# Attention with a third set of input tiles, a spread zero-fill and two-bank PSUM tiles, on one Trainium2 core

## The chip, the cores and the metric

The kernel runs on one core of one Trainium2 chip. The metric is the device time of one execution in microseconds. Of the kernel before, three runs are at hand: 874.6, 876.81 and 878.82 us, median 876.81. The engines are named TensorE (PE; PEld is its weight load), VectorE (DVE), ScalarE (ACT), GpSimd (POOL) and SyncE (SP, which here only issues transfers).

## The reference

Three stages follow one another: causal attention with a decay, a mixture of eight experts of which each token takes the best, and a dense stage. Cut to the formulas:

```python
# q, k, v: (4, 8, 576, 64), s: (4, 8, 576)
scores = q @ k.T / 8
cum    = cumsum(max(s, 0), -1)
scores = where(causal, -1e9, scores + min(-(cum[..., :, None] - cum[..., None, :]), 0))
attn   = softmax(scores)                    # exp(x - max) / (sum + 1e-9)
x      = (attn @ v) as 2304 rows of 512     # 4 batches x 576 rows

xn, en = x / (norm(x) + 1e-6), emb / (norm(emb) + 1e-6)
logits = xn @ en.T / tau                    # 8 experts
e      = argmax(logits);  gate = softmax(logits)[e]
y      = gate * (max(x @ w1[e], 0) @ w2[e])

h      = y @ w_in                           # 512 -> 2048
out    = (h * cos(h)) @ w_out               # 2048 -> 512
```

## The kernel before

**Tiling.** Attention works on 16 pairs of heads (p), four pairs to a batch. A pair is done in four steps, numbered n = 4p to 4p + 3: the last 64 query rows of both heads together, then query tiles 3, 2, and 1 with 0. A step is a chain over the engines: score matmuls on TensorE (`sco`); decay and row extreme in one pass on VectorE (`mx`, L299, which also writes `mx`); the exponential on ScalarE (`ex`, L565); transposes on TensorE into two one-bank PSUM tiles `t_ps` (`tr`, L315); a copy of one of them by ScalarE (`ca`, L571) and of the other by VectorE (`cd`, L574). Then the two products with v (`av`, L340), whose outputs are copied by ScalarE (`late`, L645) and, at the start of the next pair, by VectorE (`outs`, L610).

**Order.** In the attention part the order of SyncE, TensorE, ScalarE and VectorE is the order of the code. GpSimd's is not: a scheduler decides it when the program is built, and GpSimd then takes its instructions strictly in that order.

**Inputs.** SyncE loads q and k (`load`), the decay tile c_t (`load_c`, L107 and L109: the running sums of s, read back from `cumd` in one large and two small transfers) and v (`load_v`). Pair p + 2 is loaded in pair p; the tiles q, k and c have two buffers and v three. GpSimd then adds the causal mask to c_t in five instructions (`mask`, L129 to L134); `mx` of that pair needs them. The decay tile of pair 0 isn't loaded but made on the chip by matmuls and copies (`first_c`, tile `c_ps`).

**Rows.** When a batch's four pairs are done, `rows(b)` runs in pieces inside the next batch's loop: at each `point("a")`, `"ra"`, `"b"`, `"rb"`, `"x"` a task that waits for that name goes on by one piece. The pieces are: the logits matmuls into `lp_ps` and their copies (L388, L389), five times `turn` (transposes of the output into `r_ps`), `scaled` (a product on VectorE, L368) and `square` (ScalarE), the transposes `lt` with the products `lw` (L410), and `choose`, with the matmuls `rk` that count a token's place and the products pz. After that `route(b)` takes the norm (a power on GpSimd, L209, between two sets of VectorE operations), the gate, and for each of the five row tiles a product and a scatter to `xr` in DRAM on GpSimd (L505, L510). `xr` is zero-filled by eight transfers of 768 KB that `setup()` issues on SyncE. Batch 2's `pick_first` finds the fullest expert and loads its first rows (L539); batch 3's rows come after the loop, with `early_rows` (`xe_ps`). Then the expert stage begins, whose weights (`wraw`) are queued on SyncE behind L539.

The pools as they stand before:

```python
ld = tc.tile_pool(name="a_ld", bufs=2)                  # q, k, c; v has 3
xp = tc.tile_pool(name="a_x", bufs=7)                   # rows to scatter
ps_s = tc.tile_pool(name="ps_s", bufs=2, space=PSUM)    # two banks a tile
ps_t = tc.tile_pool(name="ps_t", bufs=4, space=PSUM)    # one bank a tile
```

Of the kernel before, what the change touches and what calls it, by code (L numbers as in the profile page):

```python
# [78 lines left out]
def attention(g, qd, kd, vd, sd, ied, embt, tau, ident, maskd, trid):  # L79
    tc, nc, const, dram, xr = g.tc, g.nc, g.const, g.dram, g.xr  # L80
    with ExitStack() as st:
        ld = st.enter_context(tc.tile_pool(name="a_ld", bufs=2))
# [6 lines left out]
        ps_t = st.enter_context(tc.tile_pool(name="ps_t", bufs=4, space=PSUM))  # L89
# [127 lines left out]
        def setup():  # L217
# [29 lines left out]
            for e in range(E):  # L247
                for _ in range(2):
                    yield
                nc.sync.dma_start(out=xr[e * NT:e * NT + 384].rearrange("(p c) d -> p c d", p=128), in_=zr.unsqueeze(1).to_broadcast([128, 3, DM]))  # L250
# [53 lines left out]
        def emit_t(n):  # L304
# [3 lines left out]
            tps = [ps_t.tile([128, 512], F32, tag="t", name="t_ps") for u in range(2)]  # L308
            for h, t in enumerate(px.pop(n)):
                for j in range(nb):  # L310
                    to = (j + 2) % 3 if tiles == (2,) else ((1, 2, 0)[j] if len(tiles) == 2 else j)
                    a = min(128 * j, S - 128) if tail else 128 * j
                    for u, tp in enumerate(tps):
                        r = slice(64 * u, 64 * u + 64)
                        nc.tensor.transpose(tp[:, 64 * (h * nb + to):64 * (h * nb + to) + 64], t[r, a:a + 128], idt[r, r])  # L315
            cp = []
            for u, tp in enumerate(tps):
                tv = tp[:, 0:128 * nb].rearrange("p (h j q) -> p h j q", h=2, j=nb) if not tail else tp[:, 0:320].rearrange("p (j q) -> p j q", j=5)
# [10 lines left out]
        def av(p, c0):  # L329
# [5 lines left out]
            o = ps_t.tile([128, 512], F32, tag="t", name="o_ps")  # L335
# [8 lines left out]
        def rows(b):  # L344
# [879 lines left out]
```

## Time and profile before

| | before |
|---|---|
| median of three runs | 876.81 us (874.6 to 878.82) |
| the profiled execution | 872.18 us |
| its span | 870.4 us |
| busy: TensorE, VectorE, ScalarE, GpSimd | 810.1, 579.0, 428.1, 129.6 us |
| TensorE busy, 0 to 200 us / 220 to 320 us | 161 of 200 / 99.2 of 100 us |
| first row load of the expert stage issued (L539) | 200.16 us |

Attention takes about the first 200 us of the span; there no engine is busy throughout. From 220 us on TensorE is. The profile comes from one execution, 4.6 us below the median, so sums of its parts are to be held against 872.2 and only their difference carried to the median. In a row of the profile's time order the bracket at the end says how long that engine had been idle before and what it then got; a row without a bracket followed at once. Rows of a few back-to-back instructions are joined (x2).

### The profile page before, as it was taken

The numbers are of one execution on the slowest core, as the hardware profiler recorded it, in microseconds if no ns is written. First come the engines' busy times: TensorE is split into PE (matmuls) and PEld (weight loads), VectorE is DVE, ScalarE is ACT, GpSimd is POOL, SyncE is SP. The second block draws the span as 40 slices with busy tenths as digits, with TensorE's granted clock in tenths as the row PEclk, the third lists the DMA queues.
The fourth block names the chain that finished last, engine by engine and source line by source line (L and its number), as shares of the span: only waits on it lengthen the run. The fifth ranks groups of instructions, "written<-read, shape, count | busy, mean of one in ns | idle before, by whom it ended". The sixth has DMA issues, their size and how long they took to land. (4 is left out here: it accounts for less than half of the span.)

```text
span 870.4 us, 14996 instructions
## 1 busy us (share of the span) xinstructions
PE 810.1 (93%) x5534; PEld 672.2 (77%) x5534; DVE 579.0 (67%) x1323; ACT 428.1 (49%) x916; POOL 129.6 (15%) x183
## 2 busy tenths in 40 slices
PE   7887989855999999999999999999999999999994
PEld 3555656534999999999998888888888888888883
DVE  5765989846456565656589968775777748544462
ACT  4776878824354454555537545343444434333331
POOL 3413474542100111111000000000000000000132
PEclk9999999975999999999999999999999999999998
DMA  6997676305976767887543212110111100000122
GB/s 209 282 377 222 209 240 208 109 36 188 328 265 150 145 151 170 173 173 151 167 156 86 95 49 73 49 49 25 49 49 49 50 0 1 1 1 0 49 85 87
DMA packets 41228, 107.84 MB, mean 124 GB/s; under 512 B 7486, under 2 KB 7998, under 8 KB 41150
## 3 DMA queue, kind: packets, MB, share of 16 engines
q1 hardware_dynamic: 37550, 97.30, 38.9%
q0 software_dynamic: 3552, 9.45, 2.9%
q8 instruction: 45, 0.74, 0.4%
q14 instruction: 33, 0.27, 0.1%
q10 hardware_dynamic: 48, 0.07, 0.0%
HBM read 91.00 MB, written 15.81 MB: 123 GB/s over the span
## 5 line engine op out<-in xcount | busy, mean ns | idle before, releaser
L804 DVE TENSOR_TENSOR wl<-wraw,wh 128x1024 fp32r<-128x1024 f32 x64 | 78.4, 1225 | 76.7 <-ACT wh L802 71.4
L1120 PE MATMUL h_ps<-x2h,wh 128*128 128x512 f32 (+1 forms) x320 | 118.4, 371 | 0.0
L1122 PE MATMUL h_ps<-x2h,wl 128*128 128x512 f32 (+1 forms) x320 | 118.3, 370 | 0.0
L1121 PE MATMUL h_ps<-x2l,wh 128*128 128x512 f32 (+1 forms) x320 | 118.1, 370 | 0.0
L1140 PE MATMUL facc<-wh,gh 128*128 128x512 f32 x288 | 114.9, 399 | 1.3 <-ACT gh L1127 1.3
L1142 PE MATMUL facc<-wh,gl 128*128 128x512 f32 x288 | 113.8, 396 | 0.0
L1141 PE MATMUL facc<-wl,gh 128*128 128x512 f32 x288 | 113.8, 395 | 0.0
L981 ACT ACTIVATE ki<-h_ps 128x512 int32<-128x512 f32 (+1 forms) x80 | 44.6, 557 | 119.6 <-PE h_ps L1122 115.0
L982 DVE SCALAR_TENSOR_TENSOR ki<-ki,h_ps 128x512 f32<-128x512 int32 (+1 forms) x80 | 50.5, 632 | 71.3 <-ACT ki L981 68.2
L802 ACT CAST wh<-wraw 128x1024 fp32r<-128x1024 f32 x64 | 67.1, 1049 | 51.2 <-PE acc L901 44.3
L565 ACT ACTIVATE s_sb<-s_sb,mx 128x576 f32<-128x576 f32 (+2 forms) x144 | 82.8, 579 | 11.0 <-DVE mx L299 10.8
L1152 POOL DMA_INDIRECT out_dram<-oacc,ti x18 | 17.5, 971 | 435.0 <-DVE oacc L1150 431.4
L901 PE MATMUL acc<-hl,wh 128*128 128x256 f32 (+7 forms) x256 | 76.7, 301 | 0.9 <-DVE hl L873 0.8
L983 ACT ACTIVATE ki<-ki,hpi 128x512 f32<-128x512 f32 (+1 forms) x80 | 54.5, 682 | 46.9 <-DVE ki L982 46.2
L902 PE MATMUL acc<-hh,wl 128*128 128x256 f32 (+7 forms) x256 | 76.5, 300 | 0.0
L900 PE MATMUL acc<-hh,wh 128*128 128x256 f32 (+7 forms) x256 | 76.3, 304 | 0.0
L1127 ACT CAST gh<-ki 128x512 fp32r<-128x512 f32 (+1 forms) x80 | 46.2, 578 | 51.6 <-DVE ki L984 51.1
L1121 PEld LDWEIGHTS h_ps<-x2l,wh 128*128 128x128 f32 x320 | 60.1, 188 | 12.5 <-DVE x2l L908 0.6
L1120 PEld LDWEIGHTS h_ps<-x2h,wh 128*128 128x128 f32 x320 | 60.0, 188 | 12.2
L1122 PEld LDWEIGHTS h_ps<-x2h,wl 128*128 128x128 f32 x320 | 60.1, 188 | 11.1
L299 DVE CUSTOM_DVE_ANT_0 s_sb<-s_ps,c_t 128x512 f32<-128x512 f32 (+3 forms) x112 | 58.3, 542 | 15.3 <-POOL c_t L129 12.8
L867 PE MATMUL h_ps<-xth,wh 128*128 128x368 f32 (+6 forms) x224 | 68.2, 304 | 0.0
(220 smaller groups left out, 1709.4 us busy)
## 6 DMA issues: line engine op xcount, KB each, us to landing
wraw<-in_wcat_dram SPq DMA_DIRECT2D x64, 512.0 KB, 4.9
wraw<-in_wf_dram SPq DMA_DIRECT2D x32, 512.0 KB, 3.6
k_t<-in_kd_dram SPq DMA_DIRECT2D x16, 496.0 KB, 4.9
c_t<-cumd SPq DMA_DIRECT2D x15, 512.0 KB
xr<-zr SPq DMA_DIRECT2D x8, 768.0 KB, 11.3
q_t<-in_qd_dram SPq DMA_DIRECT2D x16, 320.0 KB
v_t<-in_vd_dram SPq DMA_DIRECT2D x16, 320.0 KB, 6.1
c_t<-cumd SPq DMA_DIRECT2D x30, 144.0 KB, 4.7
```

What stands on the lines that cost most here:

```text
L565: nc.scalar.activation(**kw)
L804: nc.vector.tensor_tensor(out=lo, in0=raw, in1=hi.bitcast(F32), op=ALU.subtract)
L867: nc.tensor.matmul(out=ps[:, 0:c], lhsT=wh[:, sl], rhs=th[:, k, 0:c], start=(k == 0), stop=False)
L900: nc.tensor.matmul(out=ps[:, 0:c], lhsT=wh[:, sl], rhs=hh[:, 0:c], start=(f == 0), stop=False)
L901: nc.tensor.matmul(out=ps[:, 0:c], lhsT=wh[:, sl], rhs=hl[:, 0:c], start=False, stop=False)
L902: nc.tensor.matmul(out=ps[:, 0:c], lhsT=wl[:, sl], rhs=hh[:, 0:c], start=False, stop=(f == 7))
L1120: nc.tensor.matmul(out=ps[:, 0:w], lhsT=wh[:, sl], rhs=g.x2h[:, k, a0:a1], start=(k == 0), stop=False)
L1121: nc.tensor.matmul(out=ps[:, 0:w], lhsT=wh[:, sl], rhs=g.x2l[:, k, a0:a1], start=False, stop=False)
L1122: nc.tensor.matmul(out=ps[:, 0:w], lhsT=wl[:, sl], rhs=g.x2h[:, k, a0:a1], start=False, stop=(k == 3))
L1140: nc.tensor.matmul(out=acc[t], lhsT=gh[:, sl], rhs=wh[:, 512:1024], start=(c == s), stop=False)
L1141: nc.tensor.matmul(out=acc[t], lhsT=gh[:, sl], rhs=wl[:, 512:1024], start=False, stop=False)
L1142: nc.tensor.matmul(out=acc[t], lhsT=gl[:, sl], rhs=wh[:, 512:1024], start=False, stop=(c == e))
```

## The change

1. q, k and c get three buffers and v four. Pairs 1 and 2 are loaded ahead of the loop, pair p + 3 in pair p.
2. The eight zero-fills are no longer issued in two bursts by `setup()` but one each in pairs 1 to 8. A flag `g.filled` holds batch 0's route until pair 8.
3. The pool `ps_t` has two tiles of two banks in place of four of one. `c_ps`, `t_ps`, `r_ps`, `o_ps` and `xe_ps` take such a tile; `o_ps` holds both products of a pair.
4. `scaled` is one VectorE operation over both banks in place of two.
5. Two more points, `"c"` and `"rc"`; lt, lw and the pieces of `choose` move to earlier points; batch 2's `pick_first` and norm start inside pair 15.
6. The tile x has twelve buffers in place of seven.

The code, cut to its core:

```diff
-        ld = st.enter_context(tc.tile_pool(name="a_ld", bufs=2))
+        ld = st.enter_context(tc.tile_pool(name="a_ld", bufs=3))
-        ps_t = st.enter_context(tc.tile_pool(name="ps_t", bufs=4, space=PSUM))
+        ps_t = st.enter_context(tc.tile_pool(name="ps_t", bufs=2, space=PSUM))
...
-            vt[p] = ld.tile([128, 5, 128], F32, tag="v", name="v_t", bufs=3)
+            vt[p] = ld.tile([128, 5, 128], F32, tag="v", name="v_t", bufs=4)
...
         load(1)
+        load_c(1)
         load_v(0)
-        load_c(1)
+        load(2)
+        load_c(2)
         load_v(1)
+        load_v(2)
...
-            for e in range(E):
-                for _ in range(2):
-                    yield
-                nc.sync.dma_start(out=xr[e * NT:e * NT + 384]..., in_=zr...)
...
-            tps = [ps_t.tile([128, 512], F32, tag="t", name="t_ps") for u in range(2)]
+            tps = ps_t.tile([128, 2, 512], F32, tag="t", name="t_ps")
...
-                x = xs[i] = xp.tile([128, DM], F32, tag="x", name="x")
-                for h, r in enumerate(rr.pop(i)):
-                    nc.vector.tensor_tensor(...)
+                x = xs[i] = xp.tile([128, DM], F32, tag="x", name="x", bufs=12)
+                nc.vector.tensor_tensor(...)
...
-            yield "a"
+            yield "c"
             lt = ps_s.tile([128, 2, 512], F32, tag="s", name="lt_ps")
...
-            turn(2)
             square(1)
-            yield "ra"
+            yield "rc"
             lw = sm.tile([128, 5, H, E], F32, tag="lw", name="lw", bufs=1)
...
+            yield "a"
+            turn(2)
+            yield "ra"
             scaled(2)
+            lg = ...
...
+            yield "c"
+            square(3)
+            next(pick)
+            yield "rc"
+            next(pick, None)
             yield "a"
             turn(4)
             first = pick_first() if b == B - 2 else None
             if first:
                 next(first)
-            yield "rb"
+            yield "ra"
+            scaled(4)
             if first:
                 next(first)
...
-            if p + 2 < NPAIR:
-                load(p + 2)
-                load_c(p + 2)
-                load_v(p + 2)
+            if p + 3 < NPAIR:
+                load(p + 3)
+                load_c(p + 3)
+                load_v(p + 3)
+            g.filled = p >= E
+            if 0 < p <= E:
+                nc.sync.dma_start(out=xr[(p - 1) * NT:(p - 1) * NT + 384]..., in_=zr...)
...
             ca(n + 1)
+            point("c")
             tr(n + 2)
+            point("rc")
             tr(n + 3)
...
+            o2 = ps_t.tile([128, 2, 512], F32, tag="t", name="o_ps")
-            late = av(p, 256)
+            late = av(p, 256, o2)
```

How it moves instructions, at three places of the built programs. In brackets stands what an instruction waits for: an engine's name with a number is that engine's semaphore, DMAHW a transfer of SyncE's queue.

GpSimd at the start, before: c_t_114 is the decay tile of pair 0, c_t_123 that of pair 1.

```order
L129 TENSOR_TENSOR c_t_114<-c_t_114,mk_f_100 128x64 [waits DMAHW5_49,DVE_49]
L134 TENSOR_TENSOR c_t_114<-c_t_114,mk_f_100 128x256 [waits Activation_49] x2
L131 TENSOR_TENSOR c_t_114<-c_t_114,mk_f_100 128x2x128 [waits DVE_49]
L132 TENSOR_TENSOR c_t_114<-c_t_114,mk_f_100 128x2x128
L131 TENSOR_TENSOR c_t_123<-c_t_123,mk_f_100 128x2x128 [waits DMAHW1_49]
```

The same place now: c_t_114 is pair 0's, c_t_121 pair 1's and c_t_131 pair 2's.

```order
L134 TENSOR_TENSOR c_t_121<-c_t_121,mk_f_100 128x256 x2
L129 TENSOR_TENSOR c_t_121<-c_t_121,mk_f_100 128x64 [waits DMAHW2_49,DMAHW1_49]
L131 TENSOR_TENSOR c_t_131<-c_t_131,mk_f_100 128x2x128 [waits DMAHW6_49]
L132 TENSOR_TENSOR c_t_131<-c_t_131,mk_f_100 128x2x128
L134 TENSOR_TENSOR c_t_131<-c_t_131,mk_f_100 128x256
L129 TENSOR_TENSOR c_t_114<-c_t_114,mk_f_100 128x64 [waits DVE_49]
L134 TENSOR_TENSOR c_t_131<-c_t_131,mk_f_100 128x256
L129 TENSOR_TENSOR c_t_131<-c_t_131,mk_f_100 128x64 [waits DMAHW7_49,DMAHW0_49]
L134 TENSOR_TENSOR c_t_114<-c_t_114,mk_f_100 128x256 [waits Activation_49] x2
L131 TENSOR_TENSOR c_t_114<-c_t_114,mk_f_100 128x2x128 [waits DVE_49]
L132 TENSOR_TENSOR c_t_114<-c_t_114,mk_f_100 128x2x128
```

Pair 1's additions and most of pair 2's moved ahead of pair 0's.

ScalarE, the copies out of `t_ps` and of the first product in a pair of the first batch, before:

```order
L571 COPY pt<-t_ps 128x5x64 [waits PE_49,Activation_49]
L571 COPY pt<-t_ps 128x2x4x64 [waits PE_49,Activation_49]
L565 ACTIVATE s_sb,rs<-s_sb,mx 128x576 [waits DVE_49]
L571 COPY pt<-t_ps 128x2x3x64 [waits PE_49,Activation_49]
L571 COPY pu<-t_ps 128x6x64 [waits PE_49,Activation_49]
```

The same now:

```order
L576 COPY pt<-t_ps 128x5x64 [waits DVE_49,Activation_49]
L576 COPY pt<-t_ps 128x2x4x64 [waits DVE_49,Activation_49]
L570 ACTIVATE s_sb,rs<-s_sb,mx 128x576
L576 COPY pt<-t_ps 128x2x3x64 [waits DVE_49,Activation_49]
L576 COPY pu<-t_ps 128x6x64 [waits PE_49,Activation_49]
```

The order is the same, but three of the four copies wait for VectorE (its copy of the same tile) and no longer for TensorE alone; on VectorE the copy into pu and the output copies wait for ScalarE.

VectorE at the end of pair 15, before (o_ps is the last product, pf and pi belong to `pick_first`, ra to the norm of batch 2):

```order
L474 TENSOR_TENSOR cacc<-cacc,cs 128x8 [waits DVE_49]
L648 COPY ot<-o_ps 128x256 [waits PE_49]
L521 SCALAR_TENSOR_TENSOR key_3046<-c_ps,ef 128x8 [waits PE_49]
L523 TENSOR_REDUCE c_3048<-key_3046 128x1 [waits DVE_49]
L524 TENSOR_REDUCE c_3048<-c_ps 128x1
```

The same place now:

```order
L536 SCALAR_TENSOR_TENSOR pf<-pf 128x1 [waits DVE_49]
L538 CAST pi_2937<-pf 128x3 [waits DVE_49]
L212 TENSOR_SCALAR ra<-ss 128x5 [waits Activation_49]
L659 COPY ot<-o_ps 128x256 [waits Activation_49]
L216 RECIPROCAL rb<-rc 128x5 [waits Pool_49]
```

`pick_first` and the norm's first operation (on which GpSimd's power waits) moved from behind the last output copy to ahead of it.

## Rows read from the trace of the kernel before

**Rows 1.** Windows: from:to, busy by engine, granted clock, DMA share, GB/s.

```profile
80.00:100.00 20.00, 18.60 (x258) 12.70 (x256) 19.21 (x70) 17.67 (x57) 6.33 (x12) 1.00 0.59 193
```

**Rows 2.** Waits up to 180 us, VectorE then GpSimd: total, times, longest.

```profile
DVE s_sb L299 <- POOL c_t L129: 12.8, 4, 6.0
...
DVE rs L389 <- issue: 4.9, 2, 2.4
...
DVE rs L389 <- ACT lgs L388: 1.8, 1, 1.8
...
POOL c_t L131 <- DMA c_t<-cumd: 60.6, 11, 13.2
```

**Rows 3.** Time order, GpSimd: start, us, line, operation, operands, idle before.

```profile
15.63 0.73 POOL L131 TENSOR_TENSOR c_t<-c_t,mk_f 128x256 f32<-128x256 f32 x1 [1.46 <-DMA c_t<-cumd]
...
18.38 0.32 POOL L129 TENSOR_TENSOR c_t<-c_t,mk_f 128x64 f32<-128x64 f32 x1
...
25.25 0.73 POOL L131 TENSOR_TENSOR c_t<-c_t,mk_f 128x256 f32<-128x256 f32 x1 [6.55 <-DMA c_t<-cumd]
```

**Rows 4.** Time order, VectorE, pair 0, second softmax step.

```profile
14.45 0.69 DVE L299 CUSTOM_DVE_ANT_0 s_sb<-s_ps,c_t 128x512 f32<-128x512 f32 x1 [1.09 <-PE s_ps L276]
```

**Rows 5.** Time order, SyncE's queue, decay load of pair 1.

```profile
11.36 0.39 SPq L107 DMA_DIRECT2D c_t<-cumd  x1
```

**Rows 6.** DMA issues of the page: operands, count, KB each.

```profile
k_t<-in_kd_dram SPq DMA_DIRECT2D x16, 496.0 KB, 4.9
...
c_t<-cumd SPq DMA_DIRECT2D x15, 512.0 KB
...
xr<-zr SPq DMA_DIRECT2D x8, 768.0 KB, 11.3
...
q_t<-in_qd_dram SPq DMA_DIRECT2D x16, 320.0 KB
...
v_t<-in_vd_dram SPq DMA_DIRECT2D x16, 320.0 KB, 6.1
...
c_t<-cumd SPq DMA_DIRECT2D x30, 144.0 KB, 4.7
```

**Rows 7.** Two windows of 2 us, columns as in Rows 1.

```profile
22.00:24.00 2.00, 2.00 (x18) 1.30 (x18) 2.00 (x9) 2.00 (x7) 0.00 (x0) 1.00 1.04 255
...
50.00:52.00 2.00, 1.88 (x28) 1.32 (x24) 2.00 (x8) 1.91 (x5) 0.00 (x0) 1.00 1.03 401
```

**Rows 8.** Time order, VectorE, first step of pairs.

```profile
47.38 0.76 DVE L299 CUSTOM_DVE_ANT_0 s_sb<-s_ps,c_t 128x576 f32<-128x576 f32 x1 [0.44 <-ACT s_sb L565]
...
58.80 0.76 DVE L299 CUSTOM_DVE_ANT_0 s_sb<-s_ps,c_t 128x576 f32<-128x576 f32 x1 [4.05 <-POOL c_t L129]
...
72.91 0.76 DVE L299 CUSTOM_DVE_ANT_0 s_sb<-s_ps,c_t 128x576 f32<-128x576 f32 x1 [6.00 <-POOL c_t L129]
```

**Rows 9.** Time order, pair 3, copies on ScalarE and VectorE.

```profile
47.96 0.88 ACT L571 COPY pt<-t_ps 128x320 f32<-128x320 f32 x2
...
48.07 1.08 DVE L574 COPY pt<-t_ps 128x320 f32<-128x320 f32 x2
```

**Rows 10.** Time order, row stages in pairs 13 and 14.

```profile
159.59 0.64 ACT L388 COPY lgs<-lp_ps 128x576 f32<-128x576 f32 x1 [1.46 <-PE r_ps L361]
...
160.26 0.15 DVE L389 COPY rs<-lp_ps 64x4 f32<-64x4 f32 x1 [2.44 <-issue]
...
169.41 0.55 DVE L410 TENSOR_TENSOR lw<-lt_ps,ri 128x160 f32<-128x160 f32 x2 [0.16 <-PE lt_ps L404]
```

**Rows 11.** Time order, end of attention: VectorE, GpSimd, SyncE.

```profile
181.41 0.42 DVE L648 COPY ot<-o_ps 128x256 f32<-128x256 f32 x1 [2.28 <-PE o_ps L340]
...
183.37 1.20 POOL L209 TENSOR_TENSOR rc<-ra,half 128x5 f32<-128x5 f32 x1 [18.29 <-DVE ra L208]
...
192.06 0.75 DVE L368 TENSOR_TENSOR x<-r_ps,ri 64x256 f32<-64x256 f32 x2 [4.56 <-DMA xr<-x,pi]
...
200.16 1.03 SPq L539 DMA_DIRECT2D x<-xr  x2
```

More of the change, by code (lines that the diff above doesn't have):

```diff
@@ L312, in emit_t @@
                     a = min(128 * j, S - 128) if tail else 128 * j
-                    for u, tp in enumerate(tps):
+                    for u in range(2):
                         r = slice(64 * u, 64 * u + 64)
-                        nc.tensor.transpose(tp[:, 64 * (h * nb + to):64 * (h * nb + to) + 64], t[r, a:a + 128], idt[r, r])
+                        nc.tensor.transpose(tps[:, u, 64 * (h * nb + to):64 * (h * nb + to) + 64], t[r, a:a + 128], idt[r, r])
             cp = []
-            for u, tp in enumerate(tps):
-                tv = tp[:, 0:128 * nb].rearrange("p (h j q) -> p h j q", h=2, j=nb) if not tail else tp[:, 0:320].rearrange("p (j q) -> p j q", j=5)
+            for u in range(2):
+                tv = tps[:, u, 0:128 * nb].rearrange("p (h j q) -> p h j q", h=2, j=nb) if not tail else tps[:, u, 0:320].rearrange("p (j q) -> p j q", j=5)
                 if tail:
@@ L334, in av @@
             c1, last = (S, 4) if c0 else (256, 1)
-            o = ps_t.tile([128, 512], F32, tag="t", name="o_ps")
+            o = o2[:, 0 if c0 else 1]
             for j in range(last + 1):
@@ L356, in turn @@
                 q0, q1 = QT[i]
-                rr[i] = [ps_t.tile([128, 512], F32, tag="t", name="r_ps") for h in range(2)]
+                rr[i] = ps_t.tile([128, 2, 512], F32, tag="t", name="r_ps")
                 for e in range(4):
@@ L412, in rows @@
                                         in1=ri[:, :, 4 * u:4 * u + 4].unsqueeze(3).to_broadcast([128, 5, 4, E]), op=ALU.mult)
+            yield "a"
+            turn(2)
+            yield "ra"
             scaled(2)
+            lg = sm.tile(s3, F32, tag="lg", name="lg", bufs=1)
+            nc.vector.tensor_reduce(out=lg, in_=lw.rearrange("p i h e -> p i e h"), axis=AX.X, op=ALU.add)
+            nc.vector.tensor_tensor(out=l, in0=lg, in1=ien.unsqueeze(1).to_broadcast(s3), op=ALU.mult)
             yield "b"
@@ L416, in rows @@
             square(2)
-            lg = sm.tile(s3, F32, tag="lg", name="lg", bufs=1)
-            nc.vector.tensor_reduce(out=lg, in_=lw.rearrange("p i h e -> p i e h"), axis=AX.X, op=ALU.add)
-            nc.vector.tensor_tensor(out=l, in0=lg, in1=ien.unsqueeze(1).to_broadcast(s3), op=ALU.mult)
             next(pick)
@@ L423, in rows @@
             next(pick)
+            yield "c"
[3 more added lines that the diff above has]
+            next(pick, None)
             yield "a"
             turn(4)
-            square(3)
-            next(pick)
-            yield "ra"
-            scaled(4)
-            next(pick, None)
-            yield "b"
-            square(4)
             first = pick_first() if b == B - 2 else None
@@ L495, in route @@
             yield
+            while b == 0 and not g.filled:
+                yield
             gt = small([128, 5], "gt")
@@ L537, in pick_first @@
             for j in range(2):
[L538 removed]
+                x = xp.tile([128, DM], F32, tag="x", name="x", bufs=12)
                 nc.sync.dma_start(out=x, in_=xr[bass.ds(g.first * NT + 128 * j, 128)])
```

25 lines of the change are left out of this document (14 added, 11 removed).

## The prediction

> **What bounds the kernel now.** I read the table of windows first, then the waits by engine, then single stretches in time. The span is 870.4 us and the execution 872.2. Everything that the change touches lies in the first 210 us, the attention part; the expert and dense stages behind it are taken as unchanged, so the whole question is at what time they start. In the attention loop two different limits follow one another. In the pairs that carry routing rows VectorE is the limit: 19.21 of 20 us busy between 80 and 100 us [rows 1]. In the first six pairs VectorE waits: 12.8 us in four waits for GpSimd's decay additions (L129), and GpSimd in turn stood 60.6 us for the decay loads [rows 2]. So up to about 73 us the loop goes at the speed of the input queue. The reader should see that the second row explains the first: GpSimd is hardly busy, it is late because the transfer is.
>
> **Part A: what stands first on GpSimd (cost).** The order of GpSimd's work is not written by hand; in the changed program both the additions of pair 1 and the first three of pair 2 stand ahead of the first addition of pair 0, and GpSimd takes its work in order. In the kernel before, pair 1's five additions begin at 15.63 us, when its decay rows land, at about 0.7 us each, and the last, of 0.32 us, begins at 18.38 and ends at 18.70 [rows 3]. The second softmax step of pair 0 starts at 14.45 us on VectorE [rows 4]. After the change it can start only when GpSimd has: waited for pair 2's large decay transfer (landing at T); done three additions of pair 2 (2.1 us) and pair 0's 0.32; one more of pair 2 (0.7) and its 0.32, then three of pair 0 (2 x 0.7 and 0.73). That is T + 5.6 us.
> For T: behind pair 1's large decay transfer, issued at 11.36 [rows 5] and landed at 15.63, the queue now holds its two 144 KB pieces, v of pair 0 (320 KB), q, k and the large decay transfer of pair 2 (320, 496, 512 KB) [rows 6], 1,936 KB or 1.98 MB. At the 255 GB/s that these loads reached between 22 and 24 us it takes 7.8 us (T = 23.4), at the 401 GB/s of the stretch with fills 4.9 us (T = 20.5) [rows 7]. The first row is the same kind of load, but some bytes already move before 15.63: I take T = 22.5. The delay is 22.5 + 5.6 - 14.45 = **+13.7 us** (11.6 to 14.6). Nothing covers it: VectorE, ScalarE and TensorE all feed on that softmax. Even if pair 2's rows were there at once, GpSimd is occupied with pair 1 until 18.70, so the floor is 18.7 + 5.6 - 14.45 = 9.9 us.
> The Trainium skill, page "DMA: Bandwidth & Descriptors", section "Anatomy of one DMA", gives about 2 us fixed and 436 GB/s; as an estimate from that page, the 1.98 MB would take 4.5 us and T would be about 20.2. The trace's 255 GB/s under full queues speaks against it, and the sum goes by the row.
>
> **Part B: loads three pairs ahead, fill in pieces (gain).** The four VectorE waits of 12.8 us in all [rows 2], the longest 4.05 and 6.00 us before the first step of a pair [rows 8], go, since each decay load gets a whole pair more. In their place I put the 0.4 us that a pair without such a wait shows (for ScalarE, at 47.38) [rows 8]: 12.8 - 4 x 0.4 = **-11.2 us**. Does the queue keep up? From step to step those pairs take 58.80 - 47.38 - 4.05 = 7.4 and 72.91 - 58.80 - 6.00 = 8.1 us. A pair's loads are 1,936 KB, 7.8 us at 255 GB/s; a fill of 768 KB is 2.0 us at 401 GB/s [rows 6, 7]. The queue loses about 2 us a pair, in pairs 1 to 4, and has one pair (7.4 us) of lead more, plus the idle start. So it just holds; if not, up to 3 us of wait come back. Bounds -12.4 to -8.
>
> **Part C: two-bank tiles (cost).** The two halves of a transposed step were two tiles: in pair 3 ScalarE's copies at 47.96 and VectorE's at 48.07 ran side by side, 0.44 and 0.54 us each [rows 9]. With one tile of two banks the built order makes ScalarE's copy wait for VectorE's in three of four steps, the fourth the other way round, and the output copies likewise. A tile that was so before shows what that means: the copy of lp_ps on VectorE (160.26) stood 2.44 us and began once ScalarE's (159.59, 0.64 long) was through [rows 10]. By page "PSUM — Partial Sum Buffer" of the Trainium skill, section "Specifications (TRN2)", ScalarE and VectorE may read in parallel while they keep to different banks; by it the two-bank tile costs nothing. The row shows that here the program's order, not the bank, holds the reader back; the sum goes by the row.
> Laying pair 3 out again by hand, the loop of output copy, first steps, copies, four exponentials and late copy comes to 7.7 to 8.1 us instead of 7.8: +0.2 for each of five plain pairs, and +0.2 for ten pairs with rows, where ScalarE has more slack: **+3.0 us**. Bounds 0 (all covered) and one copy of each engine exposed in every pair, 16 x 0.98 = 15.7.
>
> **Part D: row pieces at other points.** The transposes lt and the products lw now follow each other with no other VectorE work between; before, lw (169.41) waited 0.16 us, [rows 10], with a copy of 0.54 us [rows 9] ahead of it as cover. Without cover that is 0.7 us, in three batches; for the rank matmuls and their products, which are fewer, I estimate 0.45, in two: **+3.0 us** (0 to 6). One scaled product of 128x512 instead of two of 128x256: two take 0.75 us together [rows 11], another operation that reads 128x512 out of PSUM 0.69 [rows 4]: -0.06 each, -1 us over twenty at most, and within the bound.
> **Part E: the end of attention (gain).** Batch 2's pick and norm now stand ahead of the last output copy. Before, GpSimd's power began at 183.37, 1.96 us behind that copy at 181.41 [rows 11]; its scatters and with them the x load on SP (200.16) follow. I take the 1.96: **-2.0 us** (-4 to 0). The 12 x buffers remove VectorE's 4.56 us wait for a scatter at 192.06 [rows 11] and two smaller ones; I cost that at nothing, because batch 3's rows run beside GpSimd's scatters and the x load, which end later; should that cover be gone, it is worth as much as it waited.
>
> **Sum**: 13.7 - 11.2 + 3.0 + 3.0 - 2.0 = +6.5 us. The profiled execution would come to 872.2 + 6.5 = 878.7. It lay 4.6 us below the median of 876.81, so for the median 883.3.
>
> **Rivals.** (1) *Pair 2's decay is there early.* If all of it lands by 18.7 us, the start costs 9.9 instead of 13.7: 879.5, no change that can be measured. For it: the queue reached 401 GB/s with other shapes. Against: before, GpSimd waited for that same transfer, queued behind the same q and k, for 6.55 us, until 25.25 [rows 3].
> (2) *The new places fit the row pairs better*, the case that isn't slower. VectorE's stalls at the first row stage, 2.44 twice and 1.8 [rows 2, 10], are 6.7 us; if the moved pieces and fewer tiles close them, part D is -6.7 instead of +3.0: 873.6. It decides against me as soon as those stalls shrink below half. Against: lp_ps is still one tile read by ScalarE first.
> (3) *The serialised readers bind every pair.* 16 x 0.98 = 15.7 in place of 3.0: 896. For it: ScalarE has the copies and the exponentials in one line, and the tile's next writer waits for both. Against: the row pairs' limit is VectorE, not ScalarE.
>
> **How the numbers follow.** My forecast has 0.42 (most of it slower, 0.06 at the edge of no change), rival 1 0.17 (0.13 no change, 0.04 slower), rival 2 0.24 (0.14 faster, 0.10 no change), rival 3 0.17 (slower). This measurement can tell about 0.5%, 4.4 us, from no change. Faster 0.14, same 0.29, slower 0.57. The range from 870 to 895 leaves out the better half of rival 2 and the worse half of rival 3.
>
> **What would show it.** Right: in the trace after, GpSimd's first wait ends with pair 2's decay near 22.5 us, the second softmax step starts near 28, no VectorE wait for L129 after that, ScalarE copies starting as VectorE's end, and the x load on SP about 4.5 us later than before. Wrong: pair 0's additions ahead of pair 2's transfer (part A falls, and the change gains about 7 us), or waits for decay rows that return in pairs 3 to 6 (part B).

## The result and the profile after

The changed kernel takes 886.73 us (median of four runs, 886.04 to 888.42) where the kernel before took 875.7 beside it: +11.0 us, ratio 1.0127 with a 95% interval of 1.0089 to 1.0165. It is slower by a little over 1%, and the whole interval lies above 1. The profiled execution took 887.13 us (span 885.3) against 872.18 before, +14.9 us; the profiled execution of before lay below its median and that of the changed kernel did not, so the profiles' difference is some 4 us more than that of the medians.

The table follows both traces from stage to stage; the times are starts in time order, of VectorE's first softmax step of a pair, of its last output copy and of SyncE's row load for the expert stage.

| | before | changed | difference |
|---|---|---|---|
| pair 1 starts | 18.74 | 30.77 | +12.0 |
| pair 1 to pair 6 | 54.17 | 46.63 | -7.5 |
| pair 6 to the last output copy | 108.50 | 120.31 | +11.8 |
| last output copy to the row load | 18.75 | 15.82 | -2.9 |
| row load starts | 200.16 | 213.53 | +13.4 |
| dense stage starts (first matmul on x2h) | 454.74 | 469.35 | +14.6 |

**The start.** These rows of the changed kernel in time order answer to [rows 3 to 5]; first GpSimd, then VectorE, then SyncE's queue.

```profile
13.76 0.72 POOL L131 TENSOR_TENSOR c_t<-c_t,mk_f 128x256 f32<-128x256 f32 x1 [11.32 <-DMA c_t<-cumd]
...
20.87 0.72 POOL L131 TENSOR_TENSOR c_t<-c_t,mk_f 128x256 f32<-128x256 f32 x1 [4.07 <-DMA c_t<-cumd]
...
22.91 0.32 POOL L129 TENSOR_TENSOR c_t<-c_t,mk_f 128x64 f32<-128x64 f32 x1
...
25.52 0.72 POOL L131 TENSOR_TENSOR c_t<-c_t,mk_f 128x256 f32<-128x256 f32 x1
...
23.27 0.76 DVE L299 CUSTOM_DVE_ANT_0 s_sb<-s_ps,c_t 128x576 f32<-128x576 f32 x1 [7.91 <-POOL c_t L129]
...
26.28 0.69 DVE L299 CUSTOM_DVE_ANT_0 s_sb<-s_ps,c_t 128x512 f32<-128x512 f32 x1 [2.24 <-POOL c_t L131]
...
10.08 0.38 SPq L107 DMA_DIRECT2D c_t<-cumd  x1
```

GpSimd stands 4.07 us for pair 2's transfer, until 20.87; only at 22.91 does it make the first addition of pair 0, and at 25.52 the one (L131) that the second step needs. VectorE waits 7.91 and 2.24 us for these two, and that step starts at 26.28 instead of 14.45.

**The waits.** Total, times and longest, up to 195 us; four rows of VectorE and one of ScalarE, to be held against [rows 2].

```profile
DVE ot L618 <- ACT ot L656: 12.6, 11, 2.4
...
DVE s_sb L299 <- POOL c_t L129: 7.9, 1, 7.9
...
DVE rs L388 <- ACT lgs L387: 4.7, 3, 1.7
...
DVE tri_b L240 <- DMA tri_f<-in_trid_dram: 3.3, 1, 3.3
...
ACT pt L576 <- DVE pt L579: 18.6, 28, 2.1
```

All of the waits for L129 that stood in the pairs are gone; the one left is that of the start. In their place stand two that the kernel before did not have: VectorE's output copy behind ScalarE's, and ScalarE's copies behind VectorE's on the same tile, 28 times. The stalls at the first row stage (L388, L389 before), 6.7 us in [rows 2], are 4.7 us here.

**The plain pairs.** Starts of pairs 4, 5 and 6 in the changed kernel, as [rows 8].

```profile
61.42 0.75 DVE L299 CUSTOM_DVE_ANT_0 s_sb<-s_ps,c_t 128x576 f32<-128x576 f32 x1
...
69.41 0.75 DVE L299 CUSTOM_DVE_ANT_0 s_sb<-s_ps,c_t 128x576 f32<-128x576 f32 x1
...
77.40 0.75 DVE L299 CUSTOM_DVE_ANT_0 s_sb<-s_ps,c_t 128x576 f32<-128x576 f32 x1
```

They follow at 7.99 us each, where 11.42 and 14.11 us lay between the same starts before.

**A pair with rows.** Pair 8 of the changed kernel in time order.

```profile
102.82 0.20 DVE L470 TENSOR_TENSOR pz<-rk_ps,eb 128x40 f32<-128x40 f32 x1 [0.40 <-PE rk_ps L467]
...
104.37 0.55 DVE L579 COPY pt<-t_ps 128x384 f32<-128x384 f32 x1
...
104.96 0.48 ACT L576 COPY pt<-t_ps 128x384 f32<-128x384 f32 x1 [1.76 <-DVE pt L579]
...
106.47 3.90 PE L340 MATMUL o_ps<-pt,v_t 128*64 128x320 f32 x20 [0.56 <-DVE pu L579]
...
111.58 0.42 DVE L618 COPY ot<-o_ps 128x256 f32<-128x256 f32 x1 [2.34 <-ACT ot L656]
```

The same stretch in windows; columns as in [rows 1].

```profile
102.00:104.00 2.00, 1.53 (x36) 1.44 (x36) 1.50 (x6) 1.20 (x4) 2.00 (x4) 1.00 1.04 352
...
104.00:106.00 2.00, 0.79 (x14) 0.44 (x10) 1.97 (x9) 1.04 (x3) 0.38 (x2) 1.00 0.68 209
...
106.00:108.00 2.00, 1.53 (x8) 0.83 (x10) 2.00 (x9) 2.00 (x7) 0.00 (x0) 0.74 0.92 362
...
108.00:110.00 2.00, 2.00 (x12) 1.05 (x10) 0.28 (x3) 1.04 (x4) 0.68 (x1) 0.50 0.38 85
```

VectorE does a piece of the routing (pz and what follows, 102.82 to 104.37; the last piece of `choose`, which the change moved to the new point `"rc"`) before its third copy of the pair. ScalarE's copy of the other half waits 1.76 us for it, and TensorE's product with v for both; TensorE is busy 0.79 of the 2 us from 104 on. The granted clock, 1.00 until then, is 0.74 and 0.50 in the next four microseconds; a stretch that was granted 0.50 ran at 1.2 of 2.4 GHz. The product takes 3.90 us (2.28 in pair 3 before), the output copies wait 2.34 us more, and the pair lasts 12.48 us instead of 8.43.

**The end.** GpSimd's power, the last output copy and the row load, as [rows 11].

```profile
196.36 1.20 POOL L213 TENSOR_TENSOR rc<-ra,half 128x5 f32<-128x5 f32 x1 [22.71 <-DVE ra L212]
...
197.71 0.42 DVE L659 COPY ot<-o_ps 128x256 f32<-128x256 f32 x1 [1.43 <-ACT ot L656]
...
213.53 0.97 SPq L544 DMA_DIRECT2D x<-xr  x2
```

The power now starts ahead of the copy, not 1.96 us behind it; the load follows the copy after 15.82 us instead of 18.75.

### The profile page after: what moved, and what is told of

The parts are those of the page before. It is cut to its first block, busy times and chain, and to the rows that moved or that the text cites. A ratio compares the mean times of both kernels' runs of the same rounds, so it can differ in the third digit from the quotient of the medians.

```text
span 885.3 us, 14973 instructions
## 1 busy us (share of the span) xinstructions
PE 810.8 (92%) x5534; PEld 668.1 (75%) x5534; DVE 583.4 (66%) x1303; ACT 429.5 (49%) x916; POOL 129.5 (15%) x183
## 5 line engine op out<-in xcount | busy, mean ns | idle before, releaser
L1151 PE MATMUL facc<-wh,gh 128*128 128x512 f32 x288 | 114.9, 399 | 1.3 <-ACT gh L1138 1.3
L1153 PE MATMUL facc<-wh,gl 128*128 128x512 f32 x288 | 113.8, 396 | 0.0
L1152 PE MATMUL facc<-wl,gh 128*128 128x512 f32 x288 | 113.8, 395 | 0.0
L570 ACT ACTIVATE s_sb<-s_sb,mx 128x576 f32<-128x576 f32 (+2 forms) x144 | 82.7, 580 | 12.7 <-DVE mx L299 12.6
L1132 PEld LDWEIGHTS h_ps<-x2l,wh 128*128 128x128 f32 x320 | 60.1, 188 | 12.4 <-DVE x2l L919 0.8
L1131 PEld LDWEIGHTS h_ps<-x2h,wh 128*128 128x128 f32 x320 | 60.0, 188 | 12.2
L1133 PEld LDWEIGHTS h_ps<-x2h,wl 128*128 128x128 f32 x320 | 60.1, 188 | 11.2
L995 DVE TENSOR_TENSOR ki<-h_ps,ki 128x512 f32<-128x512 f32 (+1 forms) x80 | 50.7, 634 | 25.7 <-ACT ki L994 24.1
```

Of the source, the lines that this page charges most:

```text
L570: nc.scalar.activation(**kw)
L1131: nc.tensor.matmul(out=ps[:, 0:w], lhsT=wh[:, sl], rhs=g.x2h[:, k, a0:a1], start=(k == 0), stop=False)
L1132: nc.tensor.matmul(out=ps[:, 0:w], lhsT=wh[:, sl], rhs=g.x2l[:, k, a0:a1], start=False, stop=False)
L1133: nc.tensor.matmul(out=ps[:, 0:w], lhsT=wl[:, sl], rhs=g.x2h[:, k, a0:a1], start=False, stop=(k == 3))
L1151: nc.tensor.matmul(out=acc[t], lhsT=gh[:, sl], rhs=wh[:, 512:1024], start=(c == s), stop=False)
L1152: nc.tensor.matmul(out=acc[t], lhsT=gh[:, sl], rhs=wl[:, 512:1024], start=False, stop=False)
```

## The experiments

Each row gives a kernel's stages from its own trace, and the ratio of its time to that of the kernel before on the same chip with the 95% interval. "Pair 6 on" is the stretch from pair 6's first step to the last output copy, "end" that from there to the row load.

| kernel | pair 1 | pair 6 | pair 6 on | end | row load | ratio |
|---|---|---|---|---|---|---|
| before | 18.74 | 72.91 | 108.50 | 18.75 | 200.16 | |
| changed | 30.77 | 77.40 | 120.31 | 15.82 | 213.53 | 1.0127 (1.0089 to 1.0165) |
| e1 changed, pair 0 first | 21.11 | 68.65 | 122.66 | 15.79 | 207.10 | 1.0082 (1.0051 to 1.0113) |
| e2 changed, one-bank tiles | 27.42 | 73.24 | 114.94 | 15.79 | 203.97 | 1.0048 (1.0015 to 1.0080) |
| e3 changed, old row pieces | 29.89 | 75.34 | 113.77 | 18.66 | 207.77 | 1.0083 (1.0048 to 1.0119) |
| f4 changed, points by name only | 29.54 | 76.92 | 124.60 | 15.79 | 217.31 | 1.0185 (1.0154 to 1.0215) |
| e4 before + loads and fill | 26.43 | 73.15 | 105.30 | 18.75 | 197.20 | 0.9973 (0.9946 to 1.0001) |
| f1 before + two-bank tiles | 25.30 | 80.49 | 111.89 | 18.74 | 211.12 | 1.0125 (1.0094 to 1.0156) |
| e10 = f1 + two points | 24.75 | 79.85 | 116.21 | 18.74 | 214.80 | 1.0161 (1.0109 to 1.0213) |
| e5 = e4 + pair 0 first | 18.72 | 64.31 | 104.62 | 18.76 | 187.69 | 0.9891 (0.9837 to 0.9945) |
| f3 = e5 + 12 x buffers | 19.68 | 67.12 | 104.20 | 18.65 | 189.97 | 0.9902 (0.9867 to 0.9937) |
| f2 = e5 + two points | 18.49 | 66.84 | 111.73 | 18.76 | 197.33 | 0.9939 (0.9903 to 0.9974) |
| e8 = e5 + 12 x buffers + two points | 18.25 | 67.75 | 110.74 | 18.68 | 197.17 | 0.9920 (0.9890 to 0.9950) |
| e9 = e5 + batch 2's norm early | 18.81 | 68.14 | 105.86 | 17.00 | 191.00 | 0.9911 (0.9883 to 0.9938) |

The kernel before took 871.6 us beside e1 to e4, 876.27 beside e5 and e8 to e10, and 875.0 beside f1 to f4; the times that the expectations name count from its 875.7 us beside the changed kernel, so they are held against the runs as differences. Each row of the table is one execution: e5, f3 and e9 have the same work up to pair 15 but for x buffers, and yet they lie 3.7 us apart from pair 1 to pair 6 and 1.7 from pair 6 on. Differences of that size are not read as effects.

My theory was that three things cost (GpSimd's order at the start, the readers of one tile, moved row pieces) and one gains (the loads); the rivals put the whole on one of them.

### Pair 0 first on GpSimd (e1)

```diff
+        mk_g = one.tile([128, 192], F32, name="mk_g")
...
+            m_f = mk_g if p else mk_f        # mask(p) adds m_f
...
         mx(0)
+        nc.vector.tensor_copy(out=mk_g, in_=mk_f)
         ex(0)
```

> The changed kernel, with one addition: the additions of pair 1 and later read a second copy of the mask, which VectorE makes behind pair 0's first softmax step. So GpSimd's order at the start is pair 0, pair 1, pair 2. Order theory (the 12 us late start comes from GpSimd's order alone): pair 0's second step is back at 14 to 15 us, and since three pairs of input are ordered early, at most 3 us of waits for L129 return; time 875 to 879. Rival (the queue of inputs is the limit and the late start only shows its wait early): the waits for L129 come back in pairs 2 to 6 with 8 us or more, time 884 to 887.

It took 876.91 us where the kernel before took 871.6 in the same comparison; e2, e3 and e4 belong to that comparison too. Its start, GpSimd and then VectorE:

```profile
15.51 0.72 POOL L132 TENSOR_TENSOR c_t<-c_t,mk_f 128x256 f32<-128x256 f32 x1 [1.09 <-DVE c_t L170]
...
16.90 0.32 POOL L130 TENSOR_TENSOR c_t<-c_t,mk_g 128x64 f32<-128x64 f32 x1
...
22.93 0.32 POOL L130 TENSOR_TENSOR c_t<-c_t,mk_g 128x64 f32<-128x64 f32 x1 [2.98 <-DMA c_t<-cumd]
...
15.04 0.39 DVE L170 COPY c_t<-c_ps 128x224 f32<-128x224 f32 x1 [2.38 <-PE c_ps L167]
...
17.17 0.69 DVE L301 CUSTOM_DVE_ANT_0 s_sb<-s_ps,c_t 128x512 f32<-128x512 f32 x1 [0.82 <-PE s_ps L278]
...
21.11 0.75 DVE L301 CUSTOM_DVE_ANT_0 s_sb<-s_ps,c_t 128x576 f32<-128x576 f32 x1
```

GpSimd is through with pair 0 before it turns to pair 1, and pair 2's transfer is awaited behind both. Pair 1 starts at 21.11 instead of 30.77, and no wait for L129 came back by pair 6 (68.65 instead of 77.40): the order is worth 9.7 us at the start and 8.8 at pair 6, and the rival of a queue that only shows its wait early falls. The time fell less (+5.3 us over the kernel before, where I had expected -0.7 to +3.3), since the stretch from pair 6 on grew by 2.3 us, with stalls in pairs 9 and 12 (13.9 and 12.8 us, 10.5 and 10.9 in the changed kernel). The code of that stretch is the same but for the second mask, so it moves by some 2 us without an edit of its own. The 2.4 us still missing to 18.74 belong to the two-bank tile `c_ps`: VectorE's copies out of it begin at 15.04 at the latest here, at 12.30 before. In e5, with one-bank tiles, pair 1 starts at 18.72.

### One-bank tiles, and the old row pieces (e2, e3)

```diff
-        ps_t = tile_pool(name="ps_t", bufs=2, space=PSUM)    # e2: two banks
+        ps_t = tile_pool(name="ps_t", bufs=4, space=PSUM)    # one bank, scaled() in two operations
```

> The changed kernel with one-bank tiles again (four buffers) for transposes, rows and outputs, and with two scaled products a tile; loads, fill, points and x buffers stay changed, and the start on GpSimd still waits for pair 2. Reader theory (ScalarE behind VectorE on one tile costs in the pairs with rows): the stretch from the first step of pair 6 to the last output copy, 120.3 us in the changed kernel and 108.5 in the kernel before, falls to 110 to 114, time 877 to 882. Rival (the moved row pieces cost it): that stretch stays within 2 us of 120, time 885 to 888.

```diff
-            yield "c"
-            lt = ps_s.tile(...)          # e3: rows() of the kernel before,
-            ...                          # from scaled(1) to route()
+            yield "a"
+            lt = ps_s.tile(...)
```

> The changed kernel with the pieces of the rows at the points of the kernel before (batch 2's pick and norm behind the loop too); two-bank tiles, loads, fill and x buffers stay changed. Reader theory: the stretch from pair 6 to the last output copy stays above 116 us, and the end loses the 3 us that the earlier norm gave; time 885 to 890. Rival (the moved pieces cost it): the stretch falls to 112 us or less; time 879 to 883.

876.34 and 879.19 us, with 871.6 before. Each of the two, undone alone, takes about half of the loss off: the stretch falls from 120.3 to 114.9 and to 113.8 us, just outside what either theory gave. So both theories were too simple, as each had one cause. Nor do the two reductions (5.4 and 6.5) tell the whole story, though their sum is near the 11.8 us lost: with both undone (e8) the stretch is still 110.7, because all three kernels kept the points c and rc; that e3's expectation names only the pieces is an omission of mine. The end goes back to 18.66 us in e3: the 2.9 us gained there come from the moved pieces.

### The loads alone (e4)

```diff
-        ld bufs=2, v bufs=3; load(p + 2) in the loop; fills in setup()
+        ld bufs=3, v bufs=4; load(p + 3) in the loop; one fill in each of pairs 1 to 8
```

> The kernel before with only the loads three pairs ahead and the fills spread over pairs 1 to 8 (parts 1 and 2 of the change); GpSimd's first additions are again held by pair 2's transfer. Order theory: late start of 11 to 13 us, less 7 to 10 us of waits for L129 that go, and rows as before: 877 to 881. Rival (the two-bank tiles or the row points are what costs in the whole, and the late start is hidden by the loads that come early): 866 to 872.

869.36 us against 871.6, ratio 0.9973. As a difference, -2.2 us lies between my theory (+1.3 to +5.3) and the rival (-9.7 to -3.7), and the late start is there as the order theory says, if smaller: 26.43 us for pair 1, 7.7 later than before. I had left out that with one-bank tiles only two of pair 0's additions, those of L131 and L132, stand behind pair 2's, and that the pairs with rows gain too: the stretch from pair 6 on is 105.3 us, 3.2 less than before. The stalls that the kernel before had in pairs 10 and 14 (12.37 and 12.22 us, 10.48 and 10.46 here) are those that go; in e5 only that of pair 14 does (11.87 and 10.67). By what way the loads or the spread fills act there was not looked into.

### The loads with pair 0 first (e5), and x buffers and tail on top (f3, e9)

The edit is that of e4 with that of e1.

> The kernel before with the loads three pairs ahead, the fills spread, and the second copy of the mask that keeps pair 0 first on GpSimd; tiles, points and x buffers as before. Order theory: pair 1 starts near 21 us, pair 6 near 68 (72.9 before), rows as in the loads-only kernel (105 us from pair 6 to the last output copy), so the x load goes out at 190 to 194 instead of 200: 6 to 9 us faster than the kernel before. Rival (the expert stage starts when its weights are there, and these are late in any case): the x load goes out early but the dense stage doesn't, less than 3 us faster.

866.54 us against 876.27 before: ratio 0.9891, -9.7 us. It beats both kernels. Pair 1 starts at 18.72 and pair 6 at 64.31; the row load goes out 12.5 us earlier than before, and the dense stage 12.2, so the rival falls.

```profile
39.23 0.20 DVE L217 RECIPROCAL rb<-rc 128x8 f32<-128x8 f32 x1 [4.16 <-POOL rc L214]
...
DVE x L369 <- DMA xr<-x,pi: 7.1, 3, 4.6
...
187.69 1.03 SPq L542 DMA_DIRECT2D x<-xr  x2
```

One late piece of work on GpSimd is left even here: in pair 2 the power of `setup()`'s norm (L214) stands behind the additions of pair 4, which begin only at 34.52, and VectorE waits 4.16 us for the power (first row; 2.51 before, 5.02 in f3 and 6.31 in e9, where GpSimd waits for pair 4's transfer). Pair 2 lasts 13.34 us, 11.10 before. It is the effect of the start once more: work of a later pair stands first.

```diff
-                x = xs[i] = xp.tile([128, DM], F32, tag="x", name="x")
+                x = xs[i] = xp.tile([128, DM], F32, tag="x", name="x", bufs=12)
```

> The kernel of e5 with twelve x buffers, and this time nothing else (e8 also had the points c and rc). VectorE's waits for scatters at the end of attention, 7.1 us in e5, vanish; if they lie beside GpSimd's chain, the stretch from the last output copy to the x load stays at 18.7 us and the time is that of e5 within 2 us; if they are on the path, 4 to 7 us less.

In e5 VectorE still waits 7.1 us for scatters (row above); with twelve buffers that wait is gone, the end is 18.65 instead of 18.76 us, and the time is the same (ratios 0.9902 and 0.9891). Those waits lay beside GpSimd's chain.

```diff
             if first:
                 next(first)
-            yield "rb"
-            if first:
                 next(first)
+            else:
+                yield "rb"
```

> The kernel of e5 with batch 2's pick and the first operation of its norm ahead of the last output copy, and no other row piece moved. If the 2.9 us that the changed kernel gained between the last output copy and the x load come from this alone, that stretch is 15.5 to 17 us (18.75 before) and the time 1 to 3 us below e5; if it needs the earlier scaled products too, it stays at 18 to 19.

The end is 17.00 instead of 18.76 us; the time, 867.08, can't be told from e5's. So some 1.8 of the 2.9 us come from the order of the pick, the norm and the last copy alone; the other 1.1 needs the rest of the moved pieces (e3 has neither).

### The two points (e8, f2)

```diff
             ca(n + 1)
+            point("c")
             tr(n + 2)
+            point("rc")
             tr(n + 3)
```

> The kernel of e5 with twelve x buffers in place of seven, and nothing else. If VectorE's 7.1 us of waits for scatters lie beside GpSimd's chain, as the prediction had it, they vanish and the x load goes out at the same time within 0.5 us; the time is that of e5 within 2 us. If they are on the path, it is 4 to 7 us faster than e5.

e8 was 3.5 us slower than e5 by the medians (the intervals of the two ratios overlap), and its stretch from pair 6 on 6.1 us longer. The expectation is wrong in its first sentence: the kernel also had the two points. At a point every task goes on that waits for that name, *and every task that waits for no name*, as the pieces of `route` do. Two more points in a pair let them run earlier.

> The kernel of e5 (loads, fill, pair 0 first on GpSimd, one-bank tiles) with the two new points c and rc in the loop and no piece named after them. If pieces that name no point now run ahead of VectorE's third copy of a pair and hold TensorE up, the pairs 8, 9, 12 and 13 show one or two stalls of 3 us and TensorE's clock at half behind them, the stretch from pair 6 to the last output copy is 108 to 112 us (104.6 in e5), and the time 3 to 7 us above e5. Rival (the stalls of e8 came from the twelve x buffers or by chance): the stretch is within 1.5 us of e5's.

f2 has the points and nothing else over e5: 870.08 against 875.0 us before (f3, beside it, 865.63), and 111.7 us from pair 6 on, 7.1 more than e5. Of these, 3.7 us are in pair 13 and 1.7 each in pairs 9 and 10; x buffers as the cause fall, since f3 has them without the loss. Pair 13 of f2 in time order, with GpSimd's additions among it:

```profile
142.47 0.73 POOL L132 TENSOR_TENSOR c_t<-c_t,mk_g 128x256 f32<-128x256 f32 x1 [1.84 <-DMA c_t<-cumd]
...
142.56 0.65 DVE L218 TENSOR_TENSOR rb<-rb,ra 128x5 f32<-128x5 f32 x1
...
143.15 0.73 POOL L133 TENSOR_TENSOR c_t<-c_t,mk_g 128x256 f32<-128x256 f32 x1
...
143.25 0.65 DVE L219 TENSOR_TENSOR rb<-rb,rc 128x5 f32<-128x5 f32 x1
...
144.62 0.19 DVE L491 RECIPROCAL nx<-nx 128x5 f32<-128x5 f32 x1
...
145.22 0.55 DVE L577 COPY pt<-t_ps 128x384 f32<-128x384 f32 x1
...
145.33 0.24 ACT L495 ACTIVATE ex<-l 128x40 f32<-128x40 f32 x1 [3.03 <-DVE l L492]
...
145.99 3.96 PE L341 MATMUL o_ps<-pt,v_t 128*64 128x320 f32 x20 [2.58 <-ACT pt L574]
```

Windows of the same stretch, then the same place in e5, with a window of it at the end.

```profile
144.00:146.00 2.00, 0.01 (x2) 0.02 (x2) 1.93 (x5) 0.67 (x3) 1.52 (x3) 1.00 0.00 0
...
146.00:148.00 2.00, 2.00 (x9) 0.91 (x11) 1.93 (x11) 2.00 (x6) 0.67 (x1) 0.55 0.03 8
...
148.00:150.00 2.00, 2.00 (x17) 1.21 (x14) 0.79 (x8) 0.92 (x5) 1.83 (x3) 0.59 0.00 0
```

```profile
136.07 0.47 ACT L574 COPY pt<-t_ps 128x384 f32<-128x384 f32 x1
...
136.22 0.55 DVE L577 COPY pt<-t_ps 128x384 f32<-128x384 f32 x1
...
137.21 2.28 PE L341 MATMUL o_ps<-pt,v_t 128*64 128x320 f32 x20
...
137.63 0.18 DVE L217 RECIPROCAL rb<-rc 128x5 f32<-128x5 f32 x1
...
140.77 0.87 PE L341 MATMUL o_ps<-pu,v_t 128*64 128x256 f32 x8 [1.28 <-DVE gt L500]
...
140.00:142.00 2.00, 1.23 (x16) 0.78 (x16) 1.93 (x12) 1.81 (x7) 0.77 (x1) 1.00 0.00 0
```

In f2 the norm's operations stand on VectorE ahead of its third copy, which comes at 145.22, 2.9 us behind the last step; ScalarE's exponential of the gate, which waits for them, stands in ScalarE's line ahead of *its* copy (3.03 us). TensorE waits 2.58 us, is granted little more than half its clock (0.55 and 0.59) and takes 3.96 us for a product that takes 2.28 in e5, where the copies come first and the norm (from 137.63) beside the product. The pair lasts 12.96 instead of 9.24 us.

### Two-bank tiles alone (e10, f1)

```diff
-        ps_t, bufs=4, [128, 512]; two scaled products a tile
+        ps_t, bufs=2, [128, 2, 512]; one scaled product a tile
```

> The kernel before with only the two-bank tiles and the single scaled product (parts 3 and 4 of the change). Reader theory: plain pairs as before within 0.2 us each, but 6 to 9 us more from pair 6 to the last output copy (108.5 before), with TensorE's clock at half behind the longest waits; the start is late too, since pair 1's additions now stand ahead of pair 0's on GpSimd, but the waits for L129 behind it shrink by as much; 6 to 10 us slower than before. Rival (two-bank tiles cost only together with the moved pieces): within 2 us of the kernel before.

> The kernel before with the two-bank tiles and the single scaled product only. It differs from the run e10 in one thing: e10 also had the two new points c and rc, at which pieces of the routing that name no point go on as well. If the readers of one tile cost by themselves, the stretch from pair 6 to the last output copy stays at 114 us or more (108.5 before, 116.2 in e10); if the two points cost it, it falls to 111 or less. Start late by 5 to 7 us as in e10; time 4 to 11 us above the kernel before.

887.91 and 884.10 us, with 876.27 and 875.0 before. By itself the tile costs 3.4 us from pair 6 on (111.89), and with the two points 7.7 (116.21). My bounds for f1 were 114 or more, or 111 or less; it came out between, so both the tiles and the points cost. (e10's own expectation doesn't name the points.) f1 also starts late, at 25.30: with a two-bank `c_ps` the scheduler puts pair 1's additions ahead of pair 0's even without any change of the loads. Its waits, total, times and longest:

```profile
DVE s_sb L300 <- POOL c_t L129: 12.2, 4, 5.1
...
DVE ot L610 <- ACT ot L646: 8.9, 8, 2.3
```

Of the waits for L129 2.4 us are the start's; in the pairs 9.8 us remain (12.8 before), and from pair 1 to pair 6 it takes 55.2 us (54.2 before). So the late start is not paid back, and the whole kernel is as slow as the changed one.

### Points that serve only named pieces (f4)

```diff
-                if t[1] in (None, at):
+                if t[1] == at or t[1] is None and at not in ("c", "rc"):
```

> The changed kernel, in which the points c and rc serve only pieces that name them; pieces of the routing that name no point go on at the old points alone. If these pieces are what stalls pairs 8, 9, 12 and 13, those four fall from 12.5, 10.5, 10.9 and 12.2 us to 9 to 10.5 each, the stretch from pair 6 to the last output copy from 120.3 to 113 to 117, and the time is 3 to 7 us below the changed kernel. Rival (two-bank readers alone): the stretch stays within 2 us of 120.

889.81 us against 875.0, and 124.6 us from pair 6 on: longer, not shorter. Pairs 8, 9, 12 and 13 took 11.1, 11.2, 12.7 and 10.4 us, so the stalls changed place rather than went, and pairs 10 and 14 rose from 11.1 and 10.8 to 12.4 and 12.4. In the kernel with one-bank tiles and old pieces the two points cost 7 us; in the changed kernel, taking the unnamed pieces off them gains nothing. The rows of VectorE in pairs 8 and 9 of f4 show why.

```profile
102.57 0.20 DVE L470 TENSOR_TENSOR pz<-rk_ps,eb 128x40 f32<-128x40 f32 x1 [0.40 <-PE rk_ps L467]
...
104.45 0.55 DVE L579 COPY pt<-t_ps 128x384 f32<-128x384 f32 x1
...
113.36 0.18 DVE L216 RECIPROCAL rb<-rc 128x5 f32<-128x5 f32 x1
...
115.57 0.55 DVE L579 COPY pt<-t_ps 128x384 f32<-128x384 f32 x1
```

In pair 8 (and 12) the piece ahead of VectorE's third copy is pz, which names `"rc"` and so stays where it was; in pair 9 it is the norm, which names no point and now goes on at an old point `"x"`, ahead of the same copy. So f4 freed that copy in neither of the two pairs, and it can't say what the points cost in the changed kernel. What a piece costs depends on which copies it falls ahead of, and where all of them would stand best with two-bank tiles stays open.

## Why the prediction came out as it did

The forecast was slower by 6.5 us, 883.3; measured are +11.0 and 886.7, within the range. By its own steps:

**Part A, right in mechanism, a little large: +13.7 forecast, +12.0 measured at pair 1.** T was 20.87 instead of 22.5. The rate was well chosen: from pair 1's landing at 13.76 to 20.87 the 1.98 MB took 7.1 us (279 GB/s; I had 255, and 7.8 us). The delay behind it was right too: the second step starts at 26.28, 5.4 us behind T, where 5.6 was forecast. What failed is the starting point: pair 1's transfer went out at 10.08 instead of 11.36 and landed at 13.76 instead of 15.63. In f1, whose loads are those of before, it lands at 15.41, so the new order of the loads brought it forward; that v of pair 0 no longer stands ahead of it is the likely reason. The estimate by the Trainium skill, page "DMA: Bandwidth & Descriptors", section "Anatomy of one DMA", 20.2, came nearer than mine, but by an accident of the two errors: its 4.5 us for those bytes would have given 18.3 from the true landing (and the page fits its figures to transfers issued from GpSimd; these are SyncE's). And e1 shows that with GpSimd's order put right 9.7 of the 12.0 us go; the 2.4 that stay belong to `c_ps`, which the sum did not have.

**Part B, mis-sized: -11.2 forecast, -7.5 measured from pair 1 to pair 6 (the readers' cost in it; the stretch scatters by up to 3.7 us between traces).** The waits for L129 went entirely and the queue kept up, as worked out. From pair 3 to pair 6 that is 33.47 us before and 23.97 now, -9.5. But pairs 1 and 2 became longer, by 1.4 and 0.6 us, though a wait for L129 of some 2.3 us in pair 1 (what [rows 2] and [rows 8] leave, less the 0.4 ahead of it) was counted as gain: in pair 1 VectorE now waits 3.3 us for `tri_f`, a small load of `setup()` that stands in the queue behind pair 3's loads (it went out at 22.39 before and at 35.26 now).

**Part C, right in size for plain pairs, too small for the others.** A plain pair lasts 7.99 us with two-bank tiles and 7.80 to 7.91 in e5, so +0.1 to +0.2, as forecast. In the pairs with rows I had +2.0; alone (f1) it is 3.4, and from e2 to the changed kernel 5.4. The failed step is "where ScalarE has more slack": what VectorE does ahead of its copy now delays ScalarE and TensorE, and in pair 8 the clock fell behind it. The page "PSUM — Partial Sum Buffer" of the Trainium skill, by whose section "Specifications (TRN2)" the tile would cost nothing, was rightly set aside: f1's row of VectorE's output copy behind ScalarE's shows a wait that is there because the program orders the two readers of one tile. The page's own statement is not contradicted by that; no run here tests it.

**Part D, the step that failed: +3.0 forecast.** From pair 6 on the changed kernel lost 11.8 us, of which parts C and D had 5.0. Going from kernel to kernel, one edit at a time: from before to f3 -4.3 (108.5 to 104.2, the loads), to e8 +6.5 (two points), to e2 +4.2 (moved pieces; e2 also lacks the second mask copy, which acts at the start), to the changed kernel +5.4 (two-bank tiles). Taken in another order the same edits have other sizes: from before to f1 +3.4 (tiles), to e10 +4.3 (points), to e3 -2.4 (loads and x buffers), to the changed kernel +6.5 (moved pieces). So the points cost 4 to 7 us in either order and the moved pieces 4 to 7, where I had 3.0. What the sum left out is a line that I had described and not priced: the two new points. I read them as places for the pieces that bear their names; the pieces of `route` that bear none also go on there. And the moved pieces I priced by the cover that they lose, 0.45 us for the rank matmuls and their products, not by the copy that they hold up: pz stands 1.55 us ahead of the third copy of pair 8. The -4.3 was missed too, since I looked for stalls that the loads remove only in the first six pairs.

**Part E, right: -2.0 forecast, -2.9 measured**, and e3 and e9 show where from: the moved pieces, 1.8 us of it the order that I had named. That the twelve x buffers are worth nothing is shown by f3.

**The sum.** At the row load 12.0 - 7.5 + 11.8 - 2.9 = +13.4 us. The remaining 1.5 us of the profile's difference come later, in the expert stage; from the row load to the dense stage the traces here show between 253 and 262 us in no order that follows the edits, so nothing is read into that. Against the forecast of 6.5 that is +2.7 up to pair 6 (B, with the plain pairs' 1.0 of part C), +6.8 from there to the last output copy (C and D), -1.7 in A and -0.9 in E; the medians say +11.0. (The sign that I gave for the row load, about 4.5 us later, doesn't follow from my own sum, all of whose 6.5 us lie ahead of that load.)

**The rivals.** Rival 1 (the transfer is there early) came half true: T was 1.6 us earlier than forecast and 2.2 later than the rival's 18.7. Rival 2 (new places fit) is refuted: the pieces at their new places cost 4.2 to 6.5 us, and the stalls at the first row stage shrank from 6.7 to 4.7 us, not below half. Rival 3 (readers bind every pair) has the right mechanism for the pairs with rows, at 3.4 to 5.4 us instead of 15.7, and the wrong one for plain pairs. That the forecast's size came near is partly luck: the cost left out (+6.5) and the gain left out (-4.3) were of opposite sign.

## What to carry to other kernels

When the loads move, look at the order of every engine whose order a scheduler decides: an in-order engine can end up waiting for tomorrow's data before it does today's work, and a data dependence (here a second copy of the mask) is a cheap way to hold it. One tile for two readers makes them one queue; here that cost 0.1 to 0.2 us a pair while nothing stood ahead of the first reader, and where a routing piece did, a stall and at times half of TensorE's clock. And of a new point in a hand-written order, list everything that may run there, not only what is named after it.

## What the runs showed of the hardware

VectorE's small operations of the norm (128x5) take 0.17 us when GpSimd is idle (L218 to L220 in pair 9 of e5) and up to 0.65 us beside its additions: in the rows of f2 above, L218 starts at 142.56 and ends at 143.21, when GpSimd's addition of 142.47 (0.73 long) ends, and L219 ends at 143.90, when the next one does. The Trainium skill, page "SBUF — State Buffer", section "SBUF: two separate sides", says that the two engines share a pair of ports under an exclusive lock, for a VectorE operation with two SBUF inputs or in a two-port mode, and that the loser waits for the whole instruction; the rows of L218 and L219, which have two inputs, agree with it to 0.02 us. The reciprocal L491, with one input, takes 0.19 us beside an addition. So six operations that last 1.25 us in pair 9 of e5 (98.35 to 99.60) held the third copy for 2.9 us in f2.

A wait of TensorE can cost more than itself: behind that of 2.58 us in f2 the next four microseconds were granted 0.55 and 0.59 of the clock and the product took 1.7 us longer. It need not: in the same pair of e5 TensorE waits 1.28 us for its second product (140.77), and the window there was granted 1.00.
